# Delta-rule attention and a GELU layer on one core: V's scalings, K's transposition and the last tile are reordered

## The chip, the core and the metric

The kernel runs on one NeuronCore of one Trainium2 chip. The core has five engines with instruction streams of their own: TensorE (PE, matrix products into PSUM), VectorE (DVE), ScalarE (ACT), GpSimd (POOL) and SyncE (SP, which here only issues transfers). They meet through semaphores. The metric is the device time of one execution in microseconds; lower is better. Before the change it is 675.7 us, the median of three runs (674.31 to 676.22).

## The reference

A delta-rule attention over 4 x 8 heads of 768 tokens and 48 dimensions is followed by a two-layer network with an exact GELU; all is float32.

```python
k_n = k / (np.linalg.norm(k, axis=-1, keepdims=True) + 1e-06)
for t in range(S):                                   # S = 768
    kt, vt, bt = (k_n[:, :, t], v[:, :, t], beta[:, :, t, None])
    y[:, :, t] = np.einsum('bhd,bhde->bhe', q[:, :, t], state)
    v_old = np.einsum('bhde,bhd->bhe', state, kt)
    state = state + bt[:, :, :, None] * np.einsum('bhd,bhe->bhde', kt, vt - v_old)
...
x = attn_out.transpose(0, 2, 1, 3).reshape(B * S, H * D)   # 3072 x 384
h = x @ w_in                                               # 384 x 2048
g = 0.5 * h * (1.0 + erf(h * inv_sqrt2))
return g @ w_out                                           # 2048 x 384
```

Line by line the recurrence has 768 dependent steps. The kernel takes it in 12 chunks of 64 tokens. Inside a chunk, the products of the keys with each other give a triangular system; VectorE eliminates it for two chunks at a time, and the rest is matrix products. The output of a chunk is then x for the network, 256 rows at a time (two tiles of 128, called a = 0 and 1).

## The kernel before

V is scaled by the norm of the keys. In most chunks GpSimd does it in one instruction per tile; for chunks 2 and 3 ScalarE does it, one instruction per head, 8 heads and 2 tiles for each chunk:

```python
    def scale_v(u, engine=nc.gpsimd):
        if u.c in (2, 3):
            for h in range(H):
                nc.scalar.mul(u.V[:, h], u.V[:, h], ns[u.c][:, u.a, h:h + 1])
            return
        engine.tensor_tensor(u.V, u.V, ns[u.c][:, u.a].unsqueeze(2).to_broadcast([128, H, D]),
                                op=ALU.mult)
```

K's transposed blocks come from VectorE, out of blocks that SyncE loaded ahead (`Kb`). psG takes the products of the keys from them, and `queries` those with the queries:

```python
    def turned_k(u):
        u.Kt = wk.tile([128, 2, NP, C], F32, tag="Kt", name="Kt", bufs=6)
        nc.vector.transpose(u.Kt.rearrange("q p j n -> q (p j n)"),
                            u.Kb.rearrange("q p j h n -> q (p j h n)"))
```

The network's first layer writes one PSUM tile psH for each of 16 columns of G, and ScalarE's GELU reads it. psH and the second layer's psO share one pool of two buffers (tag `mlp`). A finished output is sent from ScalarE's queue, one transfer for each half of the partitions:

```python
    def fc1(c, f):
        psH = ps.tile([128, NA * 128], F32, tag="mlp", name="psH")
        for m in range(NM):
            nc.tensor.matmul(psH, lhsT=w_in_sb[:, f // 2, m, f % 2 * 128:(f % 2 + 1) * 128],
                             rhs=xTs[c][:, m, :], start=(m == 0), stop=(m == NM - 1))
        nc.scalar.activation(G[:, f, :], psH, ACT.Gelu)

    def send(u):
        for p in range(2):
            row = (2 * u.a + p) * S + u.c * C
            nc.scalar.dma_start(out=out[row:row + C, :], in_=u.o[HALF[p]])

    def fc2(u, f0, f1):
        if f0 == 0:
            u.psO = ps.tile([128, DM], F32, tag="mlp", name="psO")
        for f in range(f0, f1):
            nc.tensor.matmul(u.psO, lhsT=G[:, f, u.a * 128:(u.a + 1) * 128],
                             rhs=w_out_sb[:, f, :], start=(f == 0), stop=(f == NF - 1))
        if f1 == NF:
            u.o = wk.tile([128, DM], F32, tag="o_sb", name="o_sb")
            nc.scalar.copy(u.o, u.psO)
            send(u)
```

From chunk 2 on the second layer is a product of 2 x 2 blocks in seven partial products instead of eight. It needs sums and differences of blocks of the weights, which VectorE makes once:

```python
    def sums_of_w():

        for n, a, b in ((1, B12, B11), (2, B22, 1), (4, B21, 2)):
            T[n] = more[0].tile([128, FH, DH], F32, name=f"T{n}")
            nc.vector.tensor_tensor(T[n], a, b if n == 1 else T[b], op=ALU.subtract)

    def last_sum_of_w():
        T[3] = B12
        nc.vector.tensor_tensor(B12, B22, B12, op=ALU.subtract)
```

and of blocks of G (`mix`). The seven partial products and the readings of their sums are these. The tile Y has two halves; Y[:, 0] takes the products n = 6 and 7, Y[:, 1] the last one, n = 3:

```python
    def two(c, n):
        if n == 1:
            W2["X"] = ps.tile([128, 2, DH], F32, tag="mlp", name="psX2")
            W2["o"] = [wk.tile([128, DM], F32, tag="o_sb", name="o_sb") for a in range(NA)]
            product(W2["X"][:, 0], A[0][0], B11, True)
        elif n == 5:
            W2["Z"] = small[0].tile([128, DH], F32, tag="z", name="psZ2")
            product(W2["Z"], W2["S"], T[1], True)
            W2["p1"] = more[0].tile([128, DH], F32, tag="p1", name="p1")
            nc.scalar.copy(W2["p1"], W2["X"][:, 0])
        elif n == 6:
            W2["Y"] = ps.tile([128, 2, DH], F32, tag="mlp", name="psY2")
            product(W2["Y"][:, 0], A[0][0], T[2], True)
        elif n == 2:
            product(W2["X"][:, 0], A[0][1], B21, False)
        elif n == 7:
            product(W2["Y"][:, 0], A[1][0], T[3], False)
        elif n == 4:
            product(W2["X"][:, 1], A[1][1], T[4], True)
        else:
            product(W2["Y"][:, 1], A[0][1], B22, True)

    def read2(c, n):
        o, X, Y, Z = W2["o"], W2["X"], W2["Y"], W2["Z"]
        if n == 6:
            W2["u2"] = more[0].tile([128, DH], F32, tag="u2", name="u2")
            nc.vector.tensor_tensor(W2["u2"], Y[:, 0], W2["p1"], op=ALU.add)
        elif n == 7:
            W2["u3"] = more[0].tile([128, DH], F32, tag="u3", name="u3")
            nc.vector.tensor_tensor(W2["u3"], Y[:, 0], W2["p1"], op=ALU.add)
            nc.vector.tensor_tensor(o[1][:, 0:DH], X[:, 1], W2["u3"], op=ALU.add)
            nc.vector.tensor_tensor(o[1][:, DH:], Z, W2["u3"], op=ALU.add)
            tiles[c, 1].o = o[1]
            send(tiles[c, 1])
            nc.scalar.copy(o[0][:, 0:DH], X[:, 0])
            nc.vector.tensor_tensor(W2["u2"], Z, W2["u2"], op=ALU.add)
        else:
            nc.vector.tensor_tensor(o[0][:, DH:], Y[:, 1], W2["u2"], op=ALU.add)
            tiles[c, 0].o = o[0]
            send(tiles[c, 0])
```

Steps are put in order by a list of times: `at(first, last, steps)` spreads steps over a stretch (1.0 is about one chunk), and all lists are sorted together. VectorE keeps the order of this list; the other engines' instructions are put in order by a scheduler that starts from it.

```python
    ...
    plan += [..., at(2.97, 2.971, [(1.0, finish, 4)]), ...,
             at(1.75, 2.45, eliminate_steps(1)),
             at(2.58, 2.74, join_steps(1)), at(2.72, 2.98, state_steps(2)), ...]
    plan += [at(0.995, 1.0, [(1.0, load_v, 2)]), at(2.98, 2.981, [(1.0, sums_of_w)]), at(3.1, 3.11, [(1.0, last_sum_of_w)])]
    plan += [at(max(c - 0.4, 1.66), c - 0.3, v_steps(c)) for c in range(2, NC)]
...
    for c in range(4, NC):
        t = {4: 2.73, 5: 2.98}.get(c, c - (1.97 if c % 2 == 0 else 2.36))
        plan += [at(t, t + 0.01, [(1.0, turned_k, u) for u in us])]
```

`eliminate_steps(1)` is the elimination of chunks 2 and 3 on VectorE. After it `join_run` multiplies its blocks on PE (psJ) and scales them on VectorE (XM).

Of the kernel before, what the change touches and what calls it, by code (L numbers as in the profile page):

```python
# [11 lines left out]
ALU = mybir.AluOpType  # L12
# [4 lines left out]
def kernel(  # L17
# [28 lines left out]
    nc = tc.nc  # L46
    B, H, S, D = q.shape
    DM, DF = moe_w_in.shape
    C = 64
    HB = 32  # L50
    NC = S // C
    NP = H // 2
    NA = B // 2
# [4 lines left out]
    HALF = [slice(0, C), slice(C, 2 * C)]  # L58
# [10 lines left out]
    def dn(name):  # L69
        return ps.tile([128, 2, 512], F32, tag="dn", name=name)  # L70
# [20 lines left out]
    tiles = {}  # L91
# [7 lines left out]
    for c in range(NC):  # L99
        for a in range(NA):  # L100
            u = tiles[c, a] = Unit()
# [153 lines left out]
    Ds, Gs, Nus, XMs, gms, ns = {}, {}, {}, {}, {}, {}  # L255
# [59 lines left out]
    def root(x):  # L315
# [7 lines left out]
        for i in range(3):  # L323
            nc.vector.reciprocal(r, s)
            nc.vector.tensor_tensor(r, r, x, op=ALU.mult)
            nc.vector.scalar_tensor_tensor(x if i == 2 else s, s, 0.5, r, ALU.mult, ALU.add)

    def scale_v(u, engine=nc.gpsimd):
        if u.c in (2, 3):
            for h in range(H):  # L330
                nc.scalar.mul(u.V[:, h], u.V[:, h], ns[u.c][:, u.a, h:h + 1])
            return
        engine.tensor_tensor(u.V, u.V, ns[u.c][:, u.a].unsqueeze(2).to_broadcast([128, H, D]),  # L333
                                op=ALU.mult)

# [205 lines left out]
    def v_steps(c):  # L541
        return [(1.0, scale_v, tiles[c, a]) for a in range(NA)]
# [127 lines left out]
    DH = DM // 2  # L670
    B11, B12 = w_out_sb[:, 0:FH, 0:DH], w_out_sb[:, 0:FH, DH:]
    B21, B22 = w_out_sb[:, FH:, 0:DH], w_out_sb[:, FH:, DH:]
# [6 lines left out]
                             rhs=xTs[c][:, m, :], start=(m == 0), stop=(m == NM - 1))  # L679
        nc.scalar.activation(G[:, f, :], psH, ACT.Gelu)  # L680

    def send(u):
        for p in range(2):
            row = (2 * u.a + p) * S + u.c * C
            nc.scalar.dma_start(out=out[row:row + C, :], in_=u.o[HALF[p]])

    def fc2(u, f0, f1):
        if f0 == 0:
# [8 lines that stand above are left out]
# [14 lines left out]
    A = [[G[:, k * FH:(k + 1) * FH, a * 128:(a + 1) * 128] for k in range(2)] for a in range(NA)]  # L711
    W2 = {}

    def product(ps_, lhs, rhs, first):
        for f in range(FH):
            nc.tensor.matmul(ps_, lhsT=lhs[:, f, :], rhs=rhs[:, f, :], start=first and f == 0,  # L716
                             stop=f == FH - 1, skip_group_check=not first)
# [14 lines left out]
# [17 lines that stand above are left out]
        elif n == 4:  # L749
            product(W2["X"][:, 1], A[1][1], T[4], True)  # L750
        else:
            product(W2["Y"][:, 1], A[0][1], B22, True)

    def read2(c, n):
        o, X, Y, Z = W2["o"], W2["X"], W2["Y"], W2["Z"]
# [9 lines that stand above are left out]
            send(tiles[c, 1])  # L765
            nc.scalar.copy(o[0][:, 0:DH], X[:, 0])
            nc.vector.tensor_tensor(W2["u2"], Z, W2["u2"], op=ALU.add)
        else:
            nc.vector.tensor_tensor(o[0][:, DH:], Y[:, 1], W2["u2"], op=ALU.add)
            tiles[c, 0].o = o[0]  # L770
            send(tiles[c, 0])

    def first_layer(c, f):
        fc1(c, f)
# [3 lines left out]
    def second_layer(c, n):  # L778

        two(c, n)  # L780
        if n in (1, 2):
            for h in range(2):
                mix(c, n + 1, h)
        elif n in (6, 7, 3):
            read2(c, n)

    def ffn_steps(c):
        ones = [(1.3, fc1, c, f) for f in range(NF)]
        if c > 1:
            return [(1.3, first_layer, c, f) for f in range(NF)] + [  # L790
                (2.6, second_layer, c, n) for n in (1, 5, 2, 6, 4, 7, 3)]
        twos = [(2.7, fc2, tiles[c, a], f, f + 4) for a in range(NA) for f in range(0, NF, 4)]
        if c == 0:
            twos.sort(key=lambda s: s[3])
        return ones + twos

    def at(first, last, steps):

        total, done, timed = sum(s[0] for s in steps), 0.0, []
        for w, *step in steps:  # L800
            timed.append((first + (last - first) * (done + 0.5 * w) / total, step))
            done += w
        return timed
# [78 lines left out]
    for u in first[NA:]:  # L882
        scale_v(u)
# [39 lines left out]
    plan = [at(c + 1, c + 2, ffn_steps(c)) for c in range(NC)]  # L923
# [8 lines left out]
             at(2.58, 2.74, join_steps(1)), at(2.72, 2.98, state_steps(2)),  # L932
             at(2.67, 2.671, [(1.0, prep, 4)]), at(2.8, 2.9, [(1.0, grams, [tiles[4, a] for a in range(NA)])])]
    plan += [at(0.995, 1.0, [(1.0, load_v, 2)]), at(2.98, 2.981, [(1.0, sums_of_w)]), at(3.1, 3.11, [(1.0, last_sum_of_w)])]
    plan += [at(max(c - 0.4, 1.66), c - 0.3, v_steps(c)) for c in range(2, NC)]
    plan += [at(c - 1.0, c - 0.99, [(1.0, load_v, c)]) for c in range(3, NC)]
    for c in range(4, NC):
        us = [tiles[c, a] for a in range(NA)]
        t = {4: 1.8, 5: 2.1}.get(c, c - 2.9)
        plan += [at(t, t + 0.01, [(1.0, load_blocks, c, "Kb", k)])]  # L940
        t = 3.2 if c == 4 else c - (1.3 if c % 2 == 0 else 0.9)
        plan += [at(t, t + 0.01, [(1.0, load_blocks, c, "Qb", q)])]
        t = c - (2.1 if c % 2 == 0 else 2.6) if c > 5 else {4: 2.1, 5: 2.69}[c]
        plan += [at(t, t + 0.01, [(1.0, load_k, c, "Kn")])]
        plan += [at(c - 0.4, c - 0.39, [(1.0, load_k, c, "Kp")])]
        t = {4: 2.73, 5: 2.98}.get(c, c - (1.97 if c % 2 == 0 else 2.36))
        plan += [at(t, t + 0.01, [(1.0, turned_k, u) for u in us])]
        t = c + (0.05 if c % 2 == 0 else -0.34)
        plan += [at(t, t + 0.01, [(1.0, turned_q, u) for u in us])]
# [56 lines left out]
```

## Time and profile before

| | before |
|---|---|
| median of three runs | 675.7 us |
| span of the profiled execution | 673.7 us |
| PE busy, weight loads busy | 642.2 us, 561.0 us |
| DVE, ACT, POOL busy | 452.1, 228.9, 82.1 us |
| mean granted TensorE clock | 0.966 |
| moved by DMA | 39.76 MB, mean 59 GB/s |

A profile page shows one execution. Times are in microseconds from the span's start, unless marked ns. A line such as `L680 ACT ACTIVATE G<-psH` names the line of the kernel, the engine, the operation, and what is written from what. The idle time ahead of an instruction is put down to its releaser, the work that ended last among those it waited for. PEld is the loading of weights into TensorE, which overlaps with the matmuls; a fp32 product is recorded as two matmuls, so a product over 384 rows appears six times. A name such as ACTq or SPq is the engine's queue as issuer of transfers.

How the 673.7 us lie, in 40 slices of 16.8 us, busy tenths (9 is 90% or more), with the clock that was granted to TensorE:

```profile
PE   5868998899899999999999999999999999999997
DVE  7999999985689846479846479846479844324021
PEclk9576999899999999999999999999999999999999
```

The start, where the weights are decoded and the first elimination runs on VectorE, is not full; from the thirteenth slice on PE is. The waits of ScalarE, of GpSimd and of VectorE on PE, of which the page has many, are those of engines that have less to do.

### The profile page before, as it was taken

Reading aid. Unit: us, or ns where it says so; the run is one execution under the profiler, and the core shown is the slowest. Engines: PE = TensorE matmul, PEld = TensorE weight load, DVE = VectorE, ACT = ScalarE, POOL = GpSimd, SP = SyncE. Lnnn points to the kernel's source line nnn. Section 1 sums busy time; section 2 is a strip of 40 time slices with the busy share of each in tenths; the row PEclk is TensorE's granted clock in tenths of the full one; section 3 lists DMA queues with packets and bytes.
Section 4 is the critical chain, followed back from the end, with each engine's and each line's share of the span. In section 5 each row is a group of like instructions: output and inputs, shape, how many; then the busy total and the mean of one; then the engine's idle time right before and its main releaser. Section 6 shows DMA issues by size and latency. Waiting matters only on the chain.

```text
span 673.7 us, 21703 instructions
## 1 busy us (share of the span) xinstructions
PE 642.2 (95%) x9542; PEld 561.0 (83%) x9542; DVE 452.1 (67%) x921; ACT 228.9 (34%) x605; POOL 82.1 (12%) x82
## 2 busy tenths in 40 slices
PE   5868998899899999999999999999999999999997
PEld 4656865676689989989989989989989989989996
DVE  7999999985689846479846479846479844324021
ACT  3467744614342143132143132143142132132220
POOL 4050300113011021111021111021111010000000
PEclk9576999899999999999999999999999999999999
DMA  8886555203431332511332511211301310100101
GB/s 125 186 246 177 115 173 127 47 1 67 81 45 30 57 49 49 82 31 26 58 52 45 84 29 26 53 22 32 66 3 26 55 18 3 25 1 2 24 1 25
DMA packets 158271, 39.76 MB, mean 59 GB/s; under 512 B 149984, under 2 KB 153056, under 8 KB 158176
## 3 DMA queue, kind: packets, MB, share of 16 engines
q1 hardware_dynamic: 152224, 33.26, 26.3%
q10 hardware_dynamic: 5952, 5.12, 3.3%
q8 instruction: 75, 1.23, 0.7%
q14 instruction: 20, 0.16, 0.1%
HBM read 33.62 MB, written 4.72 MB: 57 GB/s over the span
## 4 chain that ended last, share of the span: by engine, by line
PE 77%; DVE 15%; ACT 3%; issue 2%; DMA 1%; POOL 0%; SPq 0%; ACTq 0%; DVEq 0%; POOLq 0%
PE psH L678 33%; PE psY L716 12%; PE psX L716 11%; PE psZ L716 3%; PE psJ L518 3%; PE psK L573 3%; PE psG L368 3%; PE psO L691 3%; DVE Nu L445 3%; DVE tmp L443 3%; PE psU L598 2%; PE psY L616 1%; DVE w_e L235 1%; DVE w_out_sb L236 1%; PE psY L625 1%
## 5 line engine op out<-in xcount | busy, mean ns | idle before, releaser
L678 PE MATMUL psH<-xT,w_in_sb 128*128 128x256 f32 x1152 | 263.9, 386 | 4.7 <-ACT o_sb L695 2.3
L678 PEld LDWEIGHTS psH<-xT,w_in_sb 128*128 128x128 f32 x1152 | 217.8, 192 | 36.1 <-ACT o_sb L695 3.0
L680 ACT ACTIVATE G<-psH 128x256 f32<-128x256 f32 x192 | 73.4, 383 | 185.0 <-PE psH L678 173.0
L445 DVE TENSOR_TENSOR Nu<-Nu,tmp 128x30 f32<-128x30 f32 (+9 forms) x180 | 63.5, 353 | 6.2
L443 DVE TENSOR_TENSOR tmp<-Nu 128x30 f32<-128x30 f32 (+9 forms) x180 | 59.8, 332 | 5.1
L716 PE MATMUL psY<-w_out_sb,G 128*128 128x192 f32 x320 | 57.1, 330 | 1.1 <-DVE u L761 0.5
L716 PE MATMUL psX<-w_out_sb,G 128*128 128x192 f32 x320 | 56.2, 330 | 0.0
L716 PEld LDWEIGHTS psY<-w_out_sb,G 128*128 128x128 f32 x320 | 51.7, 190 | 3.1 <-DVE u L761 2.5
L716 PEld LDWEIGHTS psX<-w_out_sb,G 128*128 128x128 f32 x320 | 52.2, 190 | 0.7
L691 PE MATMUL psO<-w_out_sb,G 128*128 128x384 f32 x128 | 45.2, 496 | 1.6 <-DVE w_out_sb L236 1.6
L661 ACT COPY xT<-psX 128x384 f32<-128x384 f32 x24 | 11.4, 478 | 103.4 <-PE psX L660 103.3
L306 POOL TENSOR_TENSOR n<-n,half 128x16 f32<-128x16 f32 x10 | 29.4, 2936 | 89.1 <-DVE n L281 68.1
L691 PEld LDWEIGHTS psO<-w_out_sb,G 128*128 128x128 f32 x128 | 23.1, 190 | 16.9 <-DVE w_out_sb L236 4.0
L604 ACT COPY U<-psU 64x192 f32<-64x192 f32 x96 | 30.0, 313 | 20.0 <-PE psU L598 18.8
L403 DVE TENSOR_TENSOR P<-psG,mask 128x1024 f32<-128x1024 f32 x10 | 12.2, 1224 | 35.8 <-PE psG L368 35.8
L467 POOL MEMSET Zf<- 32x512 f32 x23 | 12.4, 540 | 153.6 <-DVE Zf L458 152.7
L725 DVE TENSOR_TENSOR S<-G 128x512 f32<-128x512 f32 x20 | 13.7, 687 | 25.8 <-ACT G L680 25.7
L581 DVE TENSOR_TENSOR W<-psK,V 128x384 f32<-128x384 f32 x22 | 12.1, 552 | 28.1 <-ACT y L580 28.1
L333 POOL TENSOR_TENSOR V<-V,n 128x384 f32<-128x384 f32 x18 | 17.2, 963 | 106.4 <-DMA V<-in_v_dram 53.2
L526 DVE TENSOR_TENSOR XM<-psJ,gm 32x512 f32<-32x512 f32 x20 | 13.8, 690 | 23.2 <-PE psJ L518 23.1
L639 DVE TENSOR_TENSOR x<-psY,y 64x192 f32<-64x192 f32 x80 | 28.3, 353 | 0.9
L716 PE MATMUL psY<-T,G 128*128 128x192 f32 x160 | 28.2, 330 | 0.0
(135 smaller groups left out, 873.6 us busy)
## 6 DMA issues: line engine op xcount, KB each, us to landing
Kp<-in_k_dram SPq DMA_DIRECT2D x76, 96.0 KB, 3.5
w_out_sb<-in_moe_w_in_dram SPq DMA_DIRECT2D x24, 256.0 KB, 4.0
V<-in_v_dram SPq DMA_DIRECT2D x48, 96.0 KB, 3.0
out_dram<-o_sb ACTq DMA_DIRECT2D x48, 96.0 KB, 2.2
w_raw<-in_moe_w_out_dram SPq DMA_DIRECT2D x10, 384.0 KB, 5.6
Zf<-in_moe_w_out_dram SPq DMA_DIRECT2D x6, 384.0 KB, 3.8
Qp<-in_q_dram SPq DMA_DIRECT2D x64, 32.0 KB, 2.3
Qp<-in_q_dram SPq DMA_DIRECT2D x16, 96.0 KB, 4.0
```

What stands on the lines that cost most here:

```text
L306: nc.gpsimd.tensor_tensor(flat, flat, half, op=ALU.pow)
L368: nc.tensor.matmul(psG[HALF[p], r, i * NP + j, :], lhsT=u.Kt[rows, p, j, :], rhs=(u.Qt if x else u.Kt)[rows, p, j, :], start=True, stop=True)
L443: nc.vector.tensor_tensor(tmp, nu[:, j + 1:, j:j + 1].to_broadcast([128, n, j]), nu[:, j:j + 1, 0:j].to_broadcast([128, n, j]), op=ALU.mult)
L445: nc.vector.tensor_tensor(nu[:, j + 1:, 0:j], nu[:, j + 1:, 0:j], tmp, op=ALU.add)
L518: nc.tensor.matmul(psJ[to, i, :], lhsT=(xm if level else off)[rows, u, :], rhs=zf[rows, u, HB:C] if level else xm[rows, u, :], start=True, ...
L573: nc.tensor.matmul(u.psK[to, x, r, j, :], lhsT=(u.Qt if x else u.Kt)[rows, p, j, :], rhs=St[rows, u.a, p, j, :], start=True, stop=True)
L604: copy(pairs(u.U[HALF[p]], s), u.psU[HALF[p ^ s], p])
L639: nc.vector.tensor_tensor(dst, src, pairs(u.y[HALF[p ^ s]], s), op=ALU.add)
L678: nc.tensor.matmul(psH, lhsT=w_in_sb[:, f // 2, m, f % 2 * 128:(f % 2 + 1) * 128], rhs=xTs[c][:, m, :], start=(m == 0), stop=(m == NM - 1))
L680: nc.scalar.activation(G[:, f, :], psH, ACT.Gelu)
L691: nc.tensor.matmul(u.psO, lhsT=G[:, f, u.a * 128:(u.a + 1) * 128], rhs=w_out_sb[:, f, :], start=(f == 0), stop=(f == NF - 1))
L716: nc.tensor.matmul(ps_, lhsT=lhs[:, f, :], rhs=rhs[:, f, :], start=first and f == 0, stop=f == FH - 1, skip_group_check=not first)
```

## The change

Three parts, with no change to what is computed.

- The 32 scalings of V of chunks 2 and 3 are no longer steps of one tile (8 in a row) at 1.66 and 2.6, but single steps, spread from 2.08 to 2.44 of the list's clock. They are meant to stand between the GELUs of that stretch and no longer ahead of the copies of psO.
- The transposition of K's blocks for chunk 5 goes from 2.98 to 2.95 of that clock, so that it stands in front of the sums of the weights (2.98).
- For the last chunk, the last partial product gets a PSUM tile of its own (psV), so that it need not wait for the reading of Y[:, 0]; and the last tile of the output is sent in two halves of its columns: the first as soon as it is complete, on SyncE's queue, the second with one transfer on SyncE's queue and one on ScalarE's.

```diff
--- before.py
+++ after.py
@@ -325,11 +325,10 @@
             nc.vector.tensor_tensor(r, r, x, op=ALU.mult)
             nc.vector.scalar_tensor_tensor(x if i == 2 else s, s, 0.5, r, ALU.mult, ALU.add)
 
+    def scale_head(u, h):
+        nc.scalar.mul(u.V[:, h], u.V[:, h], ns[u.c][:, u.a, h:h + 1])
+
     def scale_v(u, engine=nc.gpsimd):
-        if u.c in (2, 3):
-            for h in range(H):
-                nc.scalar.mul(u.V[:, h], u.V[:, h], ns[u.c][:, u.a, h:h + 1])
-            return
         engine.tensor_tensor(u.V, u.V, ns[u.c][:, u.a].unsqueeze(2).to_broadcast([128, H, D]),
                                 op=ALU.mult)
 
@@ -679,10 +678,10 @@
                              rhs=xTs[c][:, m, :], start=(m == 0), stop=(m == NM - 1))
         nc.scalar.activation(G[:, f, :], psH, ACT.Gelu)
 
-    def send(u):
+    def send(u, cols=slice(0, DM), queues=(nc.scalar, nc.scalar)):
         for p in range(2):
             row = (2 * u.a + p) * S + u.c * C
-            nc.scalar.dma_start(out=out[row:row + C, :], in_=u.o[HALF[p]])
+            queues[p].dma_start(out=out[row:row + C, cols], in_=u.o[HALF[p], cols])
 
     def fc2(u, f0, f1):
         if f0 == 0:
@@ -749,7 +748,8 @@
         elif n == 4:
             product(W2["X"][:, 1], A[1][1], T[4], True)
         else:
-            product(W2["Y"][:, 1], A[0][1], B22, True)
+            W2["V"] = W2["Y"][:, 1] if c < NC - 1 else dn("psV2")[:, 0, 0:DH]
+            product(W2["V"], A[0][1], B22, True)
 
     def read2(c, n):
         o, X, Y, Z = W2["o"], W2["X"], W2["Y"], W2["Z"]
@@ -765,10 +765,15 @@
             send(tiles[c, 1])
             nc.scalar.copy(o[0][:, 0:DH], X[:, 0])
             nc.vector.tensor_tensor(W2["u2"], Z, W2["u2"], op=ALU.add)
+            tiles[c, 0].o = o[0]
+            if c == NC - 1:
+                send(tiles[c, 0], slice(0, DH), (nc.sync, nc.sync))
         else:
-            nc.vector.tensor_tensor(o[0][:, DH:], Y[:, 1], W2["u2"], op=ALU.add)
-            tiles[c, 0].o = o[0]
-            send(tiles[c, 0])
+            nc.vector.tensor_tensor(o[0][:, DH:], W2["V"], W2["u2"], op=ALU.add)
+            if c == NC - 1:
+                send(tiles[c, 0], slice(DH, DM), (nc.sync, nc.scalar))
+            else:
+                send(tiles[c, 0])
 
     def first_layer(c, f):
         fc1(c, f)
@@ -932,7 +937,9 @@
              at(2.58, 2.74, join_steps(1)), at(2.72, 2.98, state_steps(2)),
              at(2.67, 2.671, [(1.0, prep, 4)]), at(2.8, 2.9, [(1.0, grams, [tiles[4, a] for a in range(NA)])])]
     plan += [at(0.995, 1.0, [(1.0, load_v, 2)]), at(2.98, 2.981, [(1.0, sums_of_w)]), at(3.1, 3.11, [(1.0, last_sum_of_w)])]
-    plan += [at(max(c - 0.4, 1.66), c - 0.3, v_steps(c)) for c in range(2, NC)]
+    plan += [at(c - 0.4, c - 0.3, v_steps(c)) for c in range(4, NC)]
+    plan += [at(2.08, 2.44, [(1.0, scale_head, tiles[c, a], h)
+                             for c in (2, 3) for a in range(NA) for h in range(H)])]
     plan += [at(c - 1.0, c - 0.99, [(1.0, load_v, c)]) for c in range(3, NC)]
     for c in range(4, NC):
         us = [tiles[c, a] for a in range(NA)]
@@ -943,7 +950,7 @@
         t = c - (2.1 if c % 2 == 0 else 2.6) if c > 5 else {4: 2.1, 5: 2.69}[c]
         plan += [at(t, t + 0.01, [(1.0, load_k, c, "Kn")])]
         plan += [at(c - 0.4, c - 0.39, [(1.0, load_k, c, "Kp")])]
-        t = {4: 2.73, 5: 2.98}.get(c, c - (1.97 if c % 2 == 0 else 2.36))
+        t = {4: 2.73, 5: 2.95}.get(c, c - (1.97 if c % 2 == 0 else 2.36))
         plan += [at(t, t + 0.01, [(1.0, turned_k, u) for u in us])]
         t = c + (0.05 if c % 2 == 0 else -0.34)
         plan += [at(t, t + 0.01, [(1.0, turned_q, u) for u in us])]
```

## The prediction

> **What bounds the kernel now.** I read the page first. Its busy line makes TensorE (PE) the bound:
>
> ```profile
> PE 642.2 (95%) x9542; PEld 561.0 (83%) x9542; DVE 452.1 (67%) x921; ACT 228.9 (34%) x605; POOL 82.1 (12%) x82
> ```
>
> A busy share says nothing of where the missing 5% lie, so I asked next for the waits of PE alone, once for 116 to 200 us and once for 200 to 670 us. Columns: total us, times, longest.
>
> ```profile
> PE psH L678 <- ACT o_sb L695: 2.3, 1, 2.3
> PE psG L368 <- DVE Kt L353: 1.4, 1, 1.4
> PE psH L678 <- ACT xT L661: 0.6, 1, 0.6
> ```
> ```profile
> PE psY L716 <- DVE u L761: 0.5, 1, 0.5
> ```
>
> From 200 us to the last tile PE waits once, for 0.5 us. So whatever PE gains before 200 us reaches the end whole, unless another engine then comes too late; what is gained behind the last matmul counts by itself. The three parts of the change aim at the first, the second and the fourth of these lines. For each I read the timeline around it.
>
> First, 116 to 130 us, PE and then ScalarE (start, duration, instruction, count, idle time before it):
>
> ```profile
> 116.59 2.85 PE L691 MATMUL psO<-w_out_sb,G 128*128 128x384 f32 x8 [0.48 <-DVE w_out_sb L236]
> 121.78 22.67 PE L678 MATMUL psH<-xT,w_in_sb 128*128 128x256 f32 x96 [2.35 <-ACT o_sb L695]
> ```
> ```profile
> 117.67 3.70 ACT L331 ACTIVATE V<-V,n 128x48 f32<-128x48 f32 x16
> 121.28 0.83 ACT L695 COPY o_sb<-psO 128x384 f32<-128x384 f32 x2
> 121.76 2.50 ACTq L685 DMA_DIRECT2D out_dram<-o_sb  x4
> ```
>
> The psO sums are complete at 119.44, but ScalarE works through 16 scalings of V before it copies them out, and psH needs their PSUM buffers. Behind the wait, the windows of 2 us show a second cost, the granted clock (the last three numbers are clock, DMA share, GB/s):
>
> ```profile
> 122.00:124.00 2.00, 2.00 (x8) 1.70 (x8) 1.76 (x8) 0.10 (x1) 0.00 (x0) 0.79 0.68 128
> 124.00:126.00 2.00, 2.00 (x6) 1.61 (x5) 1.83 (x6) 0.40 (x2) 0.00 (x0) 0.50 0.72 145
> ```
>
> The clock is at half in 124 to 126 us, and the stage of 96 matmul records takes 22.67 us. The same stage at 629.90 us takes 20.72 us in the chain that ended last. So this stage loses 2.35 us ahead of it and 1.95 us inside it, 4.3 us in all.
>
> Second, 178 to 186 us, PE and then VectorE:
>
> ```profile
> 179.01 4.15 PE L678 MATMUL psH<-xT,w_in_sb 128*128 128x256 f32 x18 [0.62 <-ACT xT L661]
> ...
> 185.39 0.34 PE L368 MATMUL psG<-Kt 48*64 48x64 f32 x8 [1.36 <-DVE Kt L353]
> ```
> ```profile
> 179.39 1.75 DVE L702 TENSOR_TENSOR T<-w_out_sb 128x1536 f32<-128x1536 f32 x1
> 181.17 3.55 DVE L702 TENSOR_TENSOR T<-w_out_sb,T 128x1536 f32<-128x1536 f32 x2
> 184.63 1.30 DVE L353 STREAM_TRANSPOSE Kt<-Kb 128x512 f32<-128x512 f32 x2
> ```
>
> Three weight sums, 5.33 us, stand ahead of the transposition of K that PE waits for. Its data was loaded in 117 to 127 us, so only the order holds it.
>
> Third, the end:
>
> ```profile
> 666.67 2.87 PE L716 MATMUL psY<-w_out_sb,G 128*128 128x192 f32 x16 [0.45 <-DVE u L761]
> ...
> 669.58 0.36 DVE L769 TENSOR_TENSOR o_sb<-psY,u 128x192 f32<-128x192 f32 x1 [2.04 <-PE psY L716]
> ```
>
> After it the ScalarE queue issues two transfers in a row, 1.12 us from 670.02; each lands 2.1 us after its issue.
>
> [...] The trace shows half clock right behind the gap at 119.44, [...] the shorter gaps at 112 to 116 us left it at 1.00. [...] Lines 716 and 761 do touch different columns of one tile, and PE waits 0.45 us. [...] In the trace one issue on ScalarE is 0.58 us median.
>
> **The change, part by part.**
>
> V on ScalarE. The same 32 scalings remain, and they now stand in the instruction order as 2, copy of psO, 1, two issues, copy, 1, two issues, GELU, 1, GELU, 5, GELU, 5, GELU, 4, GELU, 5, GELU, 5, GELU, 3. The memsets of Kb end at 117.76. Two scalings at 0.23 us give 118.2. The first psO, complete at about 118.0 (half of the 2.85 us), is copied by 118.7. A scaling and two issues (1.2 us) follow, and the second psO is copied by about 120.6. PE ends psO at 119.44 and starts psH at once in the first buffer, 1.3 us for one column of G; the second buffer is free when it gets there. The third needs the first GELU, which waits for two more issues until about 122.0 and ends at 122.4: some 0.45 us lost. After that each GELU has at most five scalings (1.15 us) between it and the next, against 1.3 us of matmuls, and I find about 0.1 us more. So psH would end at 119.4 + 20.7 + 0.5 = 140.6 instead of 144.4, if the clock stays full: 3.7 us gained.
>
> Not all of it is kept. VectorE's elimination does not depend on any of this, and its end doesn't move. The chain and VectorE's timeline:
>
> ```profile
> 150.75 2.78 PE psO L691 x8
> 153.52 1.22 PE psJ L518 x82
> ```
> ```profile
> 145.04 3.70 DVE L458 STREAM_TRANSPOSE Zf<-Nu 128x1024 f32<-128x1024 f32 x2
> 150.79 1.40 DVE L526 TENSOR_TENSOR XM<-psJ,gm 32x512 f32<-32x512 f32 x2 [2.05 <-PE psJ L518]
> ```
>
> The second group of psJ (153.45) reads XM. Line 526 can't start before 148.74, where the Zf transposes end; with 1.40 us it ends at 150.2. PE would come at 153.45 - 3.7 = 149.75 and wait 0.45 us. Kept: 153.45 - 150.2 = 3.2 us.
>
> K's transposition. VectorE's order becomes both transposes, then the norms, then the sums. They follow x (line 639) directly, so Kt is there by about 178.8 on the old clock, and the order on PE takes nine products of psG into the 0.62 us in which it waits for xT. Removed: the wait of 1.36 us and some 0.3 us of psG that now lies in that gap. Added: the second psT follows the first with only eleven small products between, and has to wait for its copy (0.58 us), some 0.3 us. Net 1.5 us. VectorE's sum of work up to line 403 is unchanged, 9.2 us from 177.5 to 186.7; its wait of 1.6 us there goes too, so it keeps pace with PE. The T sums are first read at 210.75.
>
> The last tile. psV in a bank of its own removes the 0.45 us. Half of the columns of the last rows go out on SyncE earlier, and the other half's two transfers start side by side on two queues: one issue of 0.56 us off the end. The bytes halve too, [...] I count nothing for it. Net 1.0 us.
>
> Sum: 3.2 + 1.5 + 1.0 = 5.7 us, so 675.7 - 5.7 = 670.0 us.
>
> **The rivals.** (a) VectorE takes over. If the waits at psJ and behind it follow VectorE more closely than I think, the first part keeps 2 us and not 3.2, and the whole is 671.2. For it: in 120 to 140 us VectorE is busy 18.28 of 20 us, and PE's slack at psJ is only 1.25 us. Against it: behind 155 us VectorE waits for PE at every join. (b) The clock falls all the same, from the gaps of 0.94 and 0.48 us before 117 us, or because the transfers of that time matter. Then the matmuls themselves are slow, the stage ends about 1.5 us later, and the time is 671.2 to 671.5. For it: the fall came some 2 us after the gap, and its cause is inferred from one place. Against it: 1.00 up to 122 us. (c) The new order of loads on SyncE (blocks of K for a later chunk now go ahead of those of q) delays a chunk. Against it: q's blocks arrive some 40 us before their use at 232.58; I give it 1 us at the very most. (d) Better than summed: the small waits at line 639 and 661 shrink, the halved transfer lands sooner, 669 or a bit less.
>
> **Range and chances.** If (a) and (b) both hold, 672.3 at most; if psJ doesn't wait at all and the end gains 1.3 us, 668.5. The three runs before lie within 2 us. I take 668.4 to 672.3. Two per cent would be 13.5 us; all PE waits that the change touches sum to under 7 us, so faster by more than 2% has a chance of 0.01. Slower by 2% would need a new wait of 19 us, which nothing in the instruction order suggests: 0.005. Within 2%: 0.985.
>
> **What would show it.** Right: no wait of psH on o_sb near 119 us, clock at 0.9 or more in 120 to 128 us, psH done near 140.6; a short wait of psJ on XM near 150; no wait of psG on Kt; line 716's last sum without a wait, and two single issues at the end on two queues. Wrong: a dip of the clock near 122 us, psJ waiting over 1 us, a wait in 200 to 660 us that wasn't there, or a last issue that lands later on SyncE's queue than on ScalarE's.

## The result and the profile after

The changed kernel takes 671.26 us, the median of 4 runs (670.63 to 671.82), against 675.88 us for the kernel before (4 runs, 674.31 to 676.22). The ratio is 0.9936, with a 95% interval of 0.9917 to 0.9955. Predicted were 670.0 us and a range of 668.4 to 672.3: the time lies in the range, and the gain is 4.6 us where 5.7 were predicted. The question for the experiments is where the missing microsecond went.

Line numbers in the changed kernel are mostly one lower than before: psH is now L677, GELU L679, psO L690, the copy into o_sb L694, psJ L517. The profiled execution spans 670.1 us. TensorE's busy line on the page:

```profile
PE 640.3 (96%) x9542; PEld 559.4 (83%) x9542; DVE 452.3 (67%) x921; ACT 228.6 (34%) x605; POOL 82.1 (12%) x82
```

TensorE has the same 9542 instructions and is still the bound. The waits of TensorE in 150 to 200 us (total us, times, longest):

```profile
PE psG L367 <- issue: 0.6, 1, 0.6
PE psX L659 <- ACT xT L660: 0.6, 1, 0.6
PE psJ L517 <- issue: 0.6, 1, 0.6
```

All four waits that the prediction showed from the kernel before, 2.3, 1.4, 0.6 and 0.5 us, are gone or have moved. Three new ones of 0.6 us stand in their place. "Issue" means that the profile shows nothing that TensorE waited for.

**The stage of psH.** TensorE's timeline of the changed kernel around 120 us:

```profile
117.38 2.85 PE L690 MATMUL psO<-w_out_sb,G 128*128 128x384 f32 x8 [0.47 <-DVE w_out_sb L236]
120.06 21.16 PE L677 MATMUL psH<-xT,w_in_sb 128*128 128x256 f32 x96
141.06 4.36 PE L690 MATMUL psO<-w_out_sb,G 128*128 128x384 f32 x13
```

There is no wait ahead of psH. The windows of 2 us (the last three numbers are granted clock, DMA share, GB/s) show the full clock (1.00) in the stretch that had 0.50; in 122 to 124 us it is 1.00 too, where it was 0.79:

```profile
124.00:126.00 2.00, 2.00 (x11) 1.76 (x10) 1.81 (x6) 1.96 (x9) 0.00 (x0) 1.00 0.46 54
```

ScalarE copies psO early, and later works through five scalings between two GELUs, 1.23 us or 246 ns each (before, 16 in a row took 3.70 us, 231 ns each):

```profile
118.97 0.48 ACT L694 COPY o_sb<-psO 128x384 f32<-128x384 f32 x1
```
```profile
123.16 1.23 ACT L329 ACTIVATE V<-V,n 128x48 f32<-128x48 f32 x5
124.42 0.38 ACT L679 ACTIVATE G<-psH 128x256 f32<-128x256 f32 x1
```

The stage ends at 141.06 us, where the next psO group starts; before, at 144.29:

```profile
144.29 5.32 PE L691 MATMUL psO<-w_out_sb,G 128*128 128x384 f32 x16
```

Single executions already differ by up to 1.3 us when they reach this place, in a part of the program that the change leaves alone: the psO group ahead of psH starts at 117.38 here, at 116.59 before and at 117.92 with part 2 alone. So I count from that start: 144.29 - 116.59 = 27.70 before, 141.06 - 117.38 = 23.68 after, 4.0 us gained.

**Behind it.** Between two psO groups lie psJ, which reads XM from VectorE, and psG. First VectorE's timeline, then TensorE's, of the changed kernel:

```profile
145.87 3.66 DVE L457 STREAM_TRANSPOSE Zf<-Nu 128x1024 f32<-128x1024 f32 x2
149.56 1.39 DVE L525 TENSOR_TENSOR XM<-psJ,gm 32x512 f32<-32x512 f32 x2
```
```profile
147.44 2.85 PE L690 MATMUL psO<-w_out_sb,G 128*128 128x384 f32 x8
...
151.06 0.18 PE L517 MATMUL psJ<-Zf,XM 32*32 32x32 f32 x1 [0.59 <-issue]
...
152.25 1.56 PE L690 MATMUL psO<-w_out_sb,G 128*128 128x384 f32 x4
153.74 0.44 PE L367 MATMUL psG<-Qt,Kt 48*64 48x64 f32 x10
154.80 1.04 PE L367 MATMUL psG<-Qt,Kt 48*64 48x64 f32 x54 [0.62 <-issue]
156.90 1.56 PE L690 MATMUL psO<-w_out_sb,G 128*128 128x384 f32 x4
```

TensorE begins psJ at 150.22, two records run, and it stops until 151.06, when XM (ended at 150.95) is there. Then, with no partner that the trace names, it stops a second time in the middle of psG. From the first psO of this fence to the last it takes 156.90 - 147.44 = 9.46 us. In the kernel before, the same stretch runs from 150.68 to 158.38, 7.70 us, with no gap:

```profile
150.68 2.85 PE L691 MATMUL psO<-w_out_sb,G 128*128 128x384 f32 x8
...
154.67 1.56 PE L691 MATMUL psO<-w_out_sb,G 128*128 128x384 f32 x4
...
158.38 1.56 PE L691 MATMUL psO<-w_out_sb,G 128*128 128x384 f32 x4
```

So 1.76 of the 4.0 us are given back here: 0.8 up to the psO group behind psJ (152.25 - 147.44 = 4.81 us against 154.67 - 150.68 = 3.99), and 0.9 from there on, where psG stops.

**K.** TensorE's timeline before and after:

```profile
177.90 0.49 PE L660 MATMUL psX<-ident,x 128*128 128x128 f32 x3
...
188.16 4.15 PE L678 MATMUL psH<-xT,w_in_sb 128*128 128x256 f32 x18
```
```profile
177.44 0.55 PE L659 MATMUL psX<-ident,x 128*128 128x128 f32 x3 [0.61 <-ACT xT L660]
...
185.84 4.37 PE L677 MATMUL psH<-xT,w_in_sb 128*128 128x256 f32 x19
```

VectorE transposes at 176.28, ahead of the three sums, and psG no longer waits. From the second psX (177.44) to the next long psH group (185.84) it takes 8.40 us; before, from 177.90 to 188.16, 10.26 us, in which two more psH records (0.44 us) were done: 1.4 us gained. The wait of 0.61 us for xT lies ahead of this count.

**The end.** The timelines of TensorE and of the two queues after:

```profile
661.27 2.76 PE L715 MATMUL psY<-w_out_sb,G 128*128 128x192 f32 x16
663.87 2.76 PE L715 MATMUL psV<-w_out_sb,G 128*128 128x192 f32 x16
```
```profile
665.12 2.44 ACTq L684 DMA_DIRECT2D out_dram<-o_sb  x3
```
```profile
665.24 2.28 SPq L684 DMA_DIRECT2D out_dram<-o_sb  x3
```

psV follows psY with no wait. From the start of psY to the end of the span it is 670.1 - 661.27 = 8.83 us; before, 673.7 - 663.46 = 10.24 us: 1.4 us gained.

### The profile page after: what moved, and what is told of

The parts are those of the page before. It is cut to its first block, busy times and chain, and to the rows that moved or that the text cites. A ratio compares the mean times of both kernels' runs of the same rounds, so it can differ in the third digit from the quotient of the medians.

```text
span 670.1 us, 21705 instructions
## 1 busy us (share of the span) xinstructions
PE 640.3 (96%) x9542; PEld 559.4 (83%) x9542; DVE 452.3 (67%) x921; ACT 228.6 (34%) x605; POOL 82.1 (12%) x82
## 3 DMA queue, kind: packets, MB, share of 16 engines
q8 instruction: 75, 1.23, 0.8%
## 4 chain that ended last, share of the span: by engine, by line
PE 82%; DVE 10%; ACT 3%; issue 2%; DMA 2%; SPq 1%; DVEq 0%; ACTq 0%
PE psH L677 36%; PE psX L715 12%; PE psY L715 12%; PE psZ L715 4%; PE psJ L517 3%; PE psK L572 3%; PE psG L367 3%; PE psO L690 2%; PE psU L597 2%; DVE Nu L444 2%; DVE tmp L442 2%; PE psY L615 1%; DVE w_e L235 1%; DVE w_out_sb L236 1%; PE psY L624 1%
## 5 line engine op out<-in xcount | busy, mean ns | idle before, releaser
L677 PE MATMUL psH<-xT,w_in_sb 128*128 128x256 f32 x1152 | 261.5, 383 | 2.3 <-ACT G L679 2.3
L677 PEld LDWEIGHTS psH<-xT,w_in_sb 128*128 128x128 f32 x1152 | 215.6, 190 | 33.7 <-ACT G L679 3.9
L679 ACT ACTIVATE G<-psH 128x256 f32<-128x256 f32 x192 | 73.3, 382 | 180.4 <-PE psH L677 168.3
L444 DVE TENSOR_TENSOR Nu<-Nu,tmp 128x30 f32<-128x30 f32 (+9 forms) x180 | 61.8, 343 | 6.2
L442 DVE TENSOR_TENSOR tmp<-Nu 128x30 f32<-128x30 f32 (+9 forms) x180 | 61.6, 342 | 5.1
L715 PE MATMUL psY<-w_out_sb,G 128*128 128x192 f32 x304 | 54.1, 329 | 0.6
L715 PEld LDWEIGHTS psY<-w_out_sb,G 128*128 128x128 f32 x304 | 49.1, 190 | 2.1 <-DVE u L761 1.8
L690 PE MATMUL psO<-w_out_sb,G 128*128 128x384 f32 x128 | 45.1, 495 | 1.6 <-DVE w_out_sb L236 1.6
L690 PEld LDWEIGHTS psO<-w_out_sb,G 128*128 128x128 f32 x128 | 23.1, 190 | 16.9 <-DVE w_out_sb L236 4.0
L715 PE MATMUL psX<-T,G 128*128 128x192 f32 x160 | 28.1, 329 | 0.0
```

Source lines behind the costliest of these rows:

```text
L442: nc.vector.tensor_tensor(tmp, nu[:, j + 1:, j:j + 1].to_broadcast([128, n, j]), nu[:, j:j + 1, 0:j].to_broadcast([128, n, j]), op=ALU.mult)
L444: nc.vector.tensor_tensor(nu[:, j + 1:, 0:j], nu[:, j + 1:, 0:j], tmp, op=ALU.add)
```

## The experiments

The ratios are to the kernel before on the same chip. A gain in microseconds is (1 - ratio) x 675.6, with its interval.

### Each part alone

The theory was that the three parts add up, and that part 1 keeps less than its 3.2 us. Part 1 alone (the changed `scale_head`, `scale_v` and `plan`):

```diff
-    plan += [at(max(c - 0.4, 1.66), c - 0.3, v_steps(c)) for c in range(2, NC)]
+    plan += [at(c - 0.4, c - 0.3, v_steps(c)) for c in range(4, NC)]
+    plan += [at(2.08, 2.44, [(1.0, scale_head, tiles[c, a], h)
+                             for c in (2, 3) for a in range(NA) for h in range(H)])]
```

> The kernel before with the first part alone: V's scalings spread between the GELUs. My theory: the 2.35 us wait of psH and the dip of the clock both go (stage psH 20.7 to 21.2 us), the stage ends 4.0 us earlier, 0.6 to 0.8 us of it is lost at psJ to VectorE's XM, and about 1 us more behind it to work whose time is set by loads; 2.2 to 3.2 us faster than before, 672.7 to 673.6. Rival, the part passes on in full: 4 us, 671.9. Rival, the clock dips again: 1.5 to 2 us, 674.

Measured: 673.67 us (11 runs), ratio 0.9977 (0.9969 to 0.9986), 1.6 us (0.9 to 2.1). The trace has psH without a wait, the full clock (1.00), and both gaps behind it (0.57 at psJ, 0.62 at psG). So the loss needs part 1 only. The gain is less than the 2.2 to 3.2 us expected: that theory had both losses behind psH about right, but took the 4.0 us against an execution with the half clock (psH in 22.67 us), which the next run shows not to come each time.

Part 2 alone:

```diff
-        t = {4: 2.73, 5: 2.98}.get(...)
+        t = {4: 2.73, 5: 2.95}.get(...)
```

> The kernel before with the second part alone: K's transposition ahead of the weight sums. My theory: no wait of psG on Kt, 1.4 to 1.7 us faster, about 674.3. Rival, VectorE's sums now come late for someone else and take the time back: 0 to 0.5 us.

Measured: 674.08 us (21 runs), ratio 0.9978 (0.9971 to 0.9985), 1.5 us (1.0 to 2.0). This kernel still has the wait of psH. Its timeline and its windows hold a surprise:

```profile
123.12 21.36 PE L678 MATMUL psH<-xT,w_in_sb 128*128 128x256 f32 x96 [2.35 <-ACT o_sb L695]
```
```profile
124.00:126.00 2.00, 1.97 (x10) 1.39 (x8) 1.79 (x7) 0.35 (x1) 0.00 (x0) 1.00 0.86 168
```

The same wait of 2.35 us, and the clock stays full, 1.00 in this window and in all others from 112 to 132 us; psH takes 21.36 us and not 22.67. So the half clock behind the wait, which the prediction counted in full, doesn't come in every execution.

Part 3 alone (psV and the two halves, as in the change):

> The kernel before with the third part alone: psV in its own bank and the last tile in two halves. My theory: 0.45 us from the bank, 0.55 us from the second issue, up to 0.4 us from the halved transfer; 1.0 to 1.4 us faster, about 674.6. Rival, a transfer issued on SyncE's queue lands later than one on ScalarE's and takes part of it back: 0.5 us.

Measured: 674.33 us (22 runs), ratio 0.9982 (0.9974 to 0.9990), 1.2 us (0.7 to 1.8). From psY to the end of its span it is 673.3 - 664.49 = 8.81 us, as in the changed kernel. Its psH group takes 22.62 us, with the clock at 0.62 and 0.52. The three gains sum to 1.6 + 1.5 + 1.2 = 4.3 us: the parts add up, and the one that falls short is the first.

### VectorE's order: the join in front of the second Zf transposition

In the changed kernel two transpositions into Zf (3.66 us) stand ahead of XM, and the second is not needed by psJ. Here only that one instruction goes behind the first pair of XM:

```diff
+    rows1 = eliminate_steps(1)
-             at(1.75, 2.45, eliminate_steps(1)),
-             at(2.58, 2.74, join_steps(1)), ...
+             at(1.75, 2.45, rows1[:-1]),
+             at(2.58, 2.74, join_steps(1)), at(2.63, 2.631, rows1[-1:]), ...
```

> The changed kernel with one VectorE instruction moved: the second Zf transposition of chunks 2 and 3 (1.85 us) goes behind the first pair of XM products. It tests whether VectorE caps the first part at psJ. My theory: XM is ready 1.8 us earlier, the wait of 0.6 to 0.7 us at the second psJ group goes, and the kernel is up to 0.6 us faster than the changed one (about 670.6) unless the next limit behind psJ takes it. Rival, the gap at psJ is instruction issue and not XM: the gap stays, same time as the changed kernel, 671.3.

Measured: 669.2 us (4 runs, 668.69 to 670.06), ratio 0.9912 (0.9899 to 0.9925), 5.9 us (5.1 to 6.8). This beats both kernels, and by more than the 0.6 us that the theory allowed over the changed one. VectorE and TensorE of this version:

```profile
145.41 1.89 DVE L457 STREAM_TRANSPOSE Zf<-Nu 128x1024 f32<-128x1024 f32 x1
147.34 1.39 DVE L525 TENSOR_TENSOR XM<-psJ,gm 32x512 f32<-32x512 f32 x2
148.76 1.94 DVE L457 STREAM_TRANSPOSE Zf<-Nu 128x1024 f32<-128x1024 f32 x1
```
```profile
147.02 2.85 PE L690 MATMUL psO<-w_out_sb,G 128*128 128x384 f32 x8
...
151.01 1.56 PE L690 MATMUL psO<-w_out_sb,G 128*128 128x384 f32 x4
152.50 1.19 PE L367 MATMUL psG<-Qt,Kt 48*64 48x64 f32 x64
154.75 1.56 PE L690 MATMUL psO<-w_out_sb,G 128*128 128x384 f32 x4
```

XM ends at 148.73, before TensorE comes for it; both gaps are gone, and the stretch takes 154.75 - 147.02 = 7.73 us again. The second gap goes with the first, although nothing of psG was touched.

The same move in the kernel before is the control:

> The kernel before with only the second Zf transposition of group 1 moved behind the first two XM products on VectorE (the move that took the changed kernel from 671.3 to 669.2 us). Theory (VectorE became the bound at psJ only because part 1 brought TensorE there earlier): the kernel before has no wait at psJ to remove, so the time stays within 0.5 us of 675.6 and psH's wait of 2.35 us is still there. Rival (the move is worth some 2 us in any kernel, so that the gain of 4.6 us was all part 1 to 3 could give): 673.6 us. The clock behind the wait of 2.35 us: half in the kernel before and with part 3 alone, full with part 2 alone, so here it may be either; the psH group then lasts 22.6 or 21.3 us.

Measured: 676.06 us (14 runs), ratio 1.0006 (0.9998 to 1.0014). Where TensorE came late, VectorE's order was worth nothing. Its profiled execution is the second one with the wait of 2.35 us and without the half clock: psH takes 21.36 us, and the clock is 1.00 in every window of 2 us from 112 to 132 us.

Its 14 times fall into two groups, three at 674.6 to 674.7 and eleven at 675.3 to 676.6; the profiled one, with the full clock, took 674.64. The kernel before has two such groups on this chip as well, 18 times at 674.4 to 675.3 and 11 at 675.7 to 676.5, so its median is lower (675.06 us). That the groups are those without and with the half clock is not shown.

### Is it XM's time, or Zf's place?

Both of these start from the version with Zf late and do one instruction twice, with the same result, so that XM is late again while Zf stays late. The first doubles the transposition into XM (2.06 us):

```diff
-             at(1.75, 2.45, rows1[:-1]),
+             at(1.75, 2.45, rows1[:-2] + rows1[-3:-1]),
```

> The version with Zf late (669.2 us), with the transposition into XM done twice, which puts 2.06 us of VectorE's work, with the same result, ahead of the first XM product again. Theory (all that the changed kernel loses behind psJ hangs on XM's time and not on Zf): XM starts at about 149.5 us again, the psJ gap of 0.6 us and the psG gap of 0.6 us come back, and the time is 671.3 us within 0.6. Rival (it was the place of Zf itself, or of its memsets on GpSimd): no gap at psG, 669.2 to 669.8 us.

Measured: 672.61 us (5 runs), ratio 0.9959 (0.9947 to 0.9972). This missed its aim: the psJ group before reads the doubled instruction's output, and the wait came there,

```profile
148.11 1.20 PE L517 MATMUL psJ<-XM,G 32*32 32x32 f32 x64 [1.78 <-DVE XM L453]
```

with no gap at psG behind it. It shows that VectorE has less than 2.06 us of slack here: 1.78 us of it became a wait. By the ratios the two versions are 3.2 us apart, more than this wait; the profiled execution was the fastest of its five, and the rest isn't explained.

The second mends it and doubles the first Zf transposition, which that psJ group doesn't read:

```diff
-             at(1.75, 2.45, rows1[:-1]),
+             at(1.75, 2.45, rows1[:-1] + rows1[-2:-1]),
```

> The version with Zf late, with the first Zf transposition of group 1 done twice: 1.9 us of VectorE's work with the same result, put ahead of the first XM product but behind the transposition that the psJ group before needs. It mends the run that doubled XM's transposition, whose wait of 1.8 us fell one psJ group too early. Theory (what the changed kernel loses behind psJ hangs on the time of the XM product): XM starts near 149.5 us, TensorE stops about 0.6 us in the second psJ group, and the time is the changed kernel's, 671.2 us within 0.6, or 2 us above the version with Zf late; the gap at psG may come back too. Rival (the order of Zf and its memsets itself): 669.2 to 669.8 us.

Measured: 671.49 us (6 runs), ratio 0.9932 (0.9917 to 0.9946). The changed kernel itself, once more on the same chip:

> The changed kernel itself once more, beside the others on one chip: 671.3 us, ratio 0.993 to 0.995. A second execution shows which of its small gaps come each time: psJ 0.6 and xT 0.6 us by the theory that both are in the program's order; the gap at psG (0.6 us in one trace, 0.2 in that with the squares on VectorE) may be absent.

Measured: 671.37 us (6 runs), ratio 0.9930 (0.9917 to 0.9944). The two are equal. In the version with the doubled Zf:

```profile
150.22 1.40 DVE L525 TENSOR_TENSOR XM<-psJ,gm 32x512 f32<-32x512 f32 x2
```
```profile
151.71 0.18 PE L517 MATMUL psJ<-Zf,XM 32*32 32x32 f32 x1 [0.84 <-issue]
```
```profile
155.09 1.04 PE L367 MATMUL psG<-Qt,Kt 48*64 48x64 f32 x54 [0.26 <-issue]
```

XM is late by the doubled instruction alone, and TensorE stops in psJ and in psG again. So the lateness of XM brings both stops, and not the place of Zf. The repeat of the changed kernel has 0.56 and 0.66 us at the two places and no wait for xT, so that third new wait was one execution's.

### The dose at psH

Part 1 alone, with twelve scalings ahead of the psO copies:

```diff
-    plan += [at(2.08, 2.44, [(1.0, scale_head, tiles[c, a], h) for c in (2, 3) ...])]
+    heads_ = [(1.0, scale_head, tiles[c, a], h) for c in (2, 3) ...]
+    plan += [at(1.66, 1.7, heads_[:12]), at(2.1, 2.44, heads_[12:])]
```

> Part 1 alone, but with twelve of V's scalings ahead of the psO copies instead of three or so, and the other twenty spread: psH waits about 1.4 us instead of 2.35 (before) or 0 (part 1 alone). Theory (behind psH VectorE is the bound, so an earlier TensorE only waits later): the wait at psH takes the place of the waits at psJ and psG, and the time is that of part 1 alone, 673.7 us within 0.5. Rival (each microsecond of psH's wait is a microsecond of the time): 675.1 us. Clock: if the half clock needs a wait as long as 2.35 us, every slice is at 1.00 behind 1.4 us; if it follows any wait, 0.5 to 0.8 for 2 to 4 us, and 676 us.

Measured: 673.78 us (15 runs), ratio 0.9980 (0.9972 to 0.9987), against 0.9977 for part 1 alone.

```profile
121.04 21.38 PE L677 MATMUL psH<-xT,w_in_sb 128*128 128x256 f32 x96 [1.45 <-ACT o_sb L694]
```
```profile
148.64 2.85 PE L690 MATMUL psO<-w_out_sb,G 128*128 128x384 f32 x8
152.63 1.56 PE L690 MATMUL psO<-w_out_sb,G 128*128 128x384 f32 x4
154.12 1.16 PE L367 MATMUL psG<-Qt,Kt 48*64 48x64 f32 x64
156.34 1.56 PE L690 MATMUL psO<-w_out_sb,G 128*128 128x384 f32 x4
```

A wait of 1.45 us ahead of psH costs nothing, because the two gaps behind it then don't come: 7.70 us for the stretch instead of 9.43. Both gaps count. Up to the psO group behind psJ, this version is 1.0 us behind part 1 alone (152.63 - 116.74 = 35.89 us from the psO group ahead of psH, against 151.97 - 117.11 = 34.86): VectorE's late XM had cost part 1 only some of the difference. At the next psO group the two are level (39.60 and 39.51 us), as the stop at psG doesn't come. The clock was 1.00 in every window of 2 us behind the 1.45 us, up to 132 us.

### ScalarE and the end

The wait for xT was still blamed on the square of chunk 6's keys, which stands ahead of the copy in ScalarE's order:

```diff
-                squares(u, n[:, u.a])
+                squares(u, n[:, u.a], nc.vector if c == 6 else None)
```

> The changed kernel with the squares of chunk 6's K on VectorE instead of ScalarE, so that no square that waits for a late load of Kp stands ahead of the copy of xT in ScalarE's order. Theory (TensorE's wait of 0.6 us for xT at 177 us is that square, and it is on the path): the wait is gone and the time is 0.4 to 0.6 us less than the changed kernel's, 670.7 us. Rival (given back at the next VectorE wait, as the two squares add 0.8 to 1 us to VectorE): 671.3 us or more.

Measured: 670.85 us (5 runs), ratio 0.9935 (0.9923 to 0.9947): no difference from the changed kernel can be told. The wait is gone, but it is gone in the repeat of the changed kernel too, so this run says nothing for the theory.

The version with Zf late, without V's 32 scalings, which are left out:

> The version with Zf late without the 32 scalings of V in chunks 2 and 3, which are left out: the most that any placing of them could bring. Theory (spread between GELUs they fit into ScalarE's idle time, and with Zf late nothing behind them waits): 669.2 us within 0.6. Rival (they still hold up GELUs or outputs and so the clock or psO): 668 us or less.

Measured: 669.70 us (5 runs), ratio 0.9906 (0.9891 to 0.9921), against 0.9912 with them. Spread between the GELUs, the scalings cost nothing that can be measured.

The kernel before with psV in a PSUM tile of its own (the expectation's bank), but the last tile sent whole:

```diff
-            product(W2["Y"][:, 1], A[0][1], B22, True)
+            W2["V"] = W2["Y"][:, 1] if c < NC - 1 else dn("psV2")[:, 0, 0:DH]
+            product(W2["V"], A[0][1], B22, True)
```

> The kernel before with psV in a bank of its own in the last chunk, but the last tile still sent whole from ScalarE. By the prediction's split of part 3: the wait of 0.45 us between psY and psV goes, the 0.56 us of the second issue stay: 0.45 us less than before, ratio 0.9993. Rival (the bank gives all of the 1.2 us that part 3 gave alone): ratio 0.998. Rival (the bank's wait was beside the last sum anyway): ratio 1.000.

Measured: 674.76 us (22 runs), ratio 0.9983 (0.9976 to 0.9990), 1.1 us (0.7 to 1.6). By the times alone the bank would give all of part 3's gain, but the two intervals (0.7 to 1.6 and 0.7 to 1.8) can't tell them apart. The traces can:

```profile
664.75 2.76 PE L716 MATMUL psY<-w_out_sb,G 128*128 128x192 f32 x16
667.35 2.76 PE L716 MATMUL psV<-w_out_sb,G 128*128 128x192 f32 x16
```

From psY to the end it is 10.24 us before, 674.3 - 664.75 = 9.55 with the bank, 8.81 with both: 0.7 us for the bank, 0.7 for the halves and queues, each from single executions.

## Why the prediction was nearly right, step by step

- **The wait of psH and its end: right.** No wait, full clock (1.00), GELUs between groups of five scalings. Counted from the psO group, 4.0 us were gained and 3.7 predicted, against an execution with the half clock. (The prediction's 140.6 and 144.4 are 3.8 us apart; its 3.7 fits the 144.29 at which the next psO group starts.)
- **The half clock: counted too often.** In the five profiled executions of kernels with the wait of 2.35 us, psH took 22.67, 22.62 and 22.67 us in three (before, part 3 alone, the bank alone) and 21.36 in two (part 2 alone, Zf late in the kernel before). In the three, the lowest window of 2 us has a clock of 0.50, 0.52 and 0.50, the one ahead of it 0.79, 0.62 and 0.66; in the two, every window has 1.00. So the half clock costs 1.3 us, three times in five: a mean of 0.8 and not 1.3, about 0.5 us less to gain, as far as five executions can say. What decides whether it comes behind this wait isn't shown.
- **"Kept: 153.45 - 150.2 = 3.2 us": right up to psJ, mis-sized behind it.** The stage did 0.3 us better than predicted, and TensorE waited for XM that much longer, so VectorE set the limit that had been worked out. From the psO group ahead of psH to the one behind psJ it is 154.67 - 116.59 = 38.08 us before and 152.25 - 117.38 = 34.87 after: 3.2 us kept, as predicted. The prediction let all of it reach the end. But the stop at psG, for which it had nothing, takes 0.9 us (41.79 and 39.52 us up to the next psO group, 2.3 kept), and the clock 0.5 us in the mean. So part 1 keeps 3.2 - 0.9 - 0.5 = 1.8 us. Alone it measured 1.6 (0.9 to 2.1). Undoing XM's lateness brought 2 us, and bringing it back by another instruction took them away.
- **K's transposition: right.** Predicted 1.5, by the trace 1.4, alone 1.5 (1.0 to 2.0).
- **The last tile: predicted 1.0,** by the trace 1.4, alone 1.2 (0.7 to 1.8). The 0.45 us of the named wait were too few for the bank: psV starts 3.21 us after psY before and 2.60 after, 0.61 us, as the end of a pipelined matmul is modelled. That the halved bytes gain nothing by themselves agrees with part 3 alone: 2.1 us to landing for 96 KB on ScalarE's queue, 2.2 us for 48 KB on SyncE's, medians of two and three transfers (2.6 and 3.0 us in the changed kernel).
- **The sum.** 1.8 + 1.4 + 1.4 = 4.6 us from single executions; 4.6 measured, 5.7 predicted. The last tile's 0.4 us more than predicted hid part of what was missing.
- **The rivals.** (a) came out in its number (part 1 keeps 2, 671.2 us), which is partly luck: the wait for VectorE at psJ cost what the main line had for it, and the rest went at psG and to the clock. (b) was false for the changed kernel; instead the clock stayed at 1.00 behind the same wait of 2.35 us in two executions of five. (c) and (d): nothing of them shows in the times.

What stays open is why TensorE stops at psG. In twelve traces with both places, the gap came in the five in which TensorE stopped inside psJ (0.62, 0.66, 0.62, 0.20 and 0.26 us) and in none of the seven others; of these, the one with XM doubled had its wait ahead of the earlier psJ group. The traces hold a possible link: before and after, the page has 75 transfers of instructions on a queue q8, 1.23 MB or 16 KB each, and one of them begins ahead of psG. This is the DMA rate in 150 to 158 us, one number for each 0.2 us, first before, then after; each 82 (16 KB in 0.2 us) is such a transfer:

```profile
GB/s 0 0 0 0 0 0 0 0 0 0 0 0 0 0 0 0 82 0 0 0 0 0 0 0 0 0 0 0 0 0 0 0 0 0 0 82 0 0 0 0
GB/s 0 0 0 0 0 0 0 0 0 0 82 0 0 0 0 0 0 0 0 0 0 0 0 0 0 0 0 0 0 82 0 29 143 192 98 43 121 120 104 84
```

Before, it begins at 153.39, 2.77 us ahead of psG's first record (156.16); after, at 152.04, only 1.70 us ahead, behind the stop in psJ (which ends at 151.06). By the same series, in the seven traces without the gap it is 2.3 to 3.0 us ahead, in the five with it 1.3 to 1.7, and there TensorE goes on, always at the eleventh record, 2.1 to 2.8 us after the transfer began. At 17.08 us before and 17.52 us after, a stop in psG of 1.85 and 1.14 us ends 3.1 and 2.4 us after such a transfer began. psG may have waited for its instructions; no run moved the transfer alone, and this isn't shown.

## What to carry to other kernels

When a wait on the bounding engine is taken away, work out how much slack the next engine has at the next meeting point; if little, move what that meeting doesn't need behind it in the same change. One transposition moved on VectorE was worth 2 us here, and nothing at all before the first wait was gone. A stop can also cost more than itself: 0.8 us at psJ brought 0.9 us more at psG. And before a clock dip is counted as a gain, look at it in more than one execution: here it came in three of five.

## What was not expected of the hardware

- After the same wait of 2.35 us the granted clock fell to 0.50 to 0.52 in a window of 2 us in three executions (psH 22.62 to 22.67 us) and stayed at 1.00 in two (21.36 us); after 1.45 us it stayed at 1.00 in the one profiled (21.38 us). What decides it isn't shown.
- In five traces a stop of 0.6 to 0.8 us inside a group of small matmuls is followed, 3 to 4 us later, by a second one of 0.2 to 0.7 us in another group, for which the profile names no partner. The second ends 2.1 to 2.8 us after a transfer of instructions began.
